# Fused attention and MLP block on one core: sequence rows 4p+j, loads in waves, and a new instruction order

## The chip, the cores and the metric

The kernel runs on 1 core of one Trainium2 chip. The metric is the device time of one execution in microseconds (us). Repeated executions of one kernel give a median and a range; each profiled execution also gives a span (first to last instruction, about 2 us less than the time) and the mean clock that was granted to TensorE. Engine names: PE is TensorE, PEld its weight loads, DVE VectorE, ACT ScalarE, POOL GpSimd, SP SyncE, which issues most DMAs.

## The reference

One transformer block on 2048 rows of 512 features, in bf16, with 32 heads. Each position attends to 8 positions: itself and those 2, 4, ... 14 before it.

```python
h   = x + attention(layernorm(x), wqkv) @ wo        # window 8, dilation 2
out = h + ((relu(n @ W_gate) * (n @ W_up)) @ W_down)  # n = layernorm(h), 1376 hidden features
```

## The kernel before

The rows are worked on in four chunks of 512. A chunk is loaded as four blocks of 128 rows, normalised, and transposed, so that the projections give q, k and v with the features on partitions and the positions along the free axis. The kernel adds all instructions to a plan; a list of ranks (tuned elsewhere) then fixes their order on every engine.

```python
x_rows   = A_x.rearrange("b (tb p) d -> p (b tb) d", p=P)        # block of 128 successive rows
out_rows = out.rearrange("b (tb p) d -> p (b tb) d", p=P)
...
kT = sb.tile([P, NT, PADL + S], BF16, name="kT")     # keys of all chunks in one tile, 16 columns of zeros ahead
vT = sb.tile([P, NT, PADL + S], BF16, name="vT")
...
# setup: every load is issued at once
for j in range(BPC):
    (nc.scalar if j % 2 else nc.sync).dma_start(x_sm[:, j:j + 1, :], x_rows[:, j:j + 1, :])
for c, q in enumerate((nc.sync, nc.scalar, nc.sync)):
    q.dma_start(w3_sb[c][:], w3_r[:, :, c * D:(c + 1) * D])
for tk in range(1, NCK):
    nc.sync.dma_start(x_sm[:, tk * BPC:(tk + 1) * BPC, :], x_rows[:, tk * BPC:(tk + 1) * BPC, :])
...
def f_ev(...):                       # eviction of a projection, 12 in each chunk, 48 in all
    if c == 0:
        o = qT.t[:, t, :]
    else:
        o = (kT if c == 1 else vT)[:, t, PADL + s0: PADL + s0 + CS]
    nc.scalar.copy(out=o, in_=mm.t[:])
...
def f_pr(...):                       # one score product: 2 feature tiles x 4 window positions x 512
    kb = kT[:, t:t + 2, PADL + s0 - 4 * hf * DIL: PADL + s0 - 4 * hf * DIL + CS]
    ...
    V.tensor_tensor(out=pb.t[:]..., in0=q4, in1=k4, op=ALU.mult)
```

The softmax here doesn't subtract the row's maximum and nothing guards it: scores larger than these inputs give would overflow.

## Time and profile before

| | |
|---|---|
| time, first three runs | 203.12 us (202.84 to 203.56) |
| time of the profiled execution | 205.38 us, span 203.6, clock 0.983 |
| the 48 projection evictions | 0.60 us each |

Beside the lines that the prediction shows, these two views matter later. The first is the page's busy times and the slices of ScalarE (40 equal slices, tenths of busy time):

```profile
PE 195.4 (96%) x1102; PEld 96.8 (48%) x1123; DVE 155.1 (76%) x246; ACT 127.7 (63%) x253; POOL 12.6 (6%) x26
...
ACT  3517879986569993797756599703665353576400
```

The second is the groups of the projection evictions (count, busy us and mean ns of one, idle time before them and its releaser):

```profile
L519 ACT CAST quad<-bank 128x512 bf16<-128x512 f32 x16 | 9.6, 601 | 7.4 <-PE bank L511 7.4
L519 ACT CAST vT<-bank 128x512 bf16<-128x512 f32 x16 | 9.5, 600 | 2.3 <-PE bank L511 2.3
L519 ACT CAST kT<-bank 128x512 bf16<-128x512 f32 x16 | 9.4, 599 | 3.3 <-PE bank L511 3.3
```

ScalarE is busy 63% on average, but several slices of the first half stand at 9.

### The profile page before, as it was taken

The numbers are of one execution on the slowest core, as the hardware profiler recorded it, in microseconds if no ns is written. First come the engines' busy times: TensorE is split into PE (matmuls) and PEld (weight loads), VectorE is DVE, ScalarE is ACT, GpSimd is POOL, SyncE is SP. The second block draws the span as 40 slices with busy tenths as digits, with TensorE's granted clock in tenths as the row PEclk, the third lists the DMA queues.
The fourth block names the chain that finished last, engine by engine and source line by source line (L and its number), as shares of the span: only waits on it lengthen the run. The fifth ranks groups of instructions, "written<-read, shape, count | busy, mean of one in ns | idle before, by whom it ended". The sixth has DMA issues, their size and how long they took to land.

```text
span 203.6 us, 2957 instructions
## 1 busy us (share of the span) xinstructions
PE 195.4 (96%) x1102; PEld 96.8 (48%) x1123; DVE 155.1 (76%) x246; ACT 127.7 (63%) x253; POOL 12.6 (6%) x26
## 2 busy tenths in 40 slices
PE   8499999999999999999999999999999999999994
PEld 8347545555545334444454444444444445444452
DVE  6549999999999999999999966599996255021314
ACT  3517879986569993797756599703665353576400
POOL 3000000330000002400033000000000000000000
PEclk9859999999999999999999999999999999999999
DMA  5999901698000002980059900400011001100003
GB/s 187 350 379 403 322 19 30 123 203 163 3 0 0 0 3 52 192 168 0 3 103 180 209 31 0 90 13 0 3 41 62 0 0 53 53 0 0 0 3 103
DMA packets 14893, 18.04 MB, mean 89 GB/s; under 512 B 5056, under 2 KB 12192, under 8 KB 14880
## 3 DMA queue, kind: packets, MB, share of 16 engines
q1 hardware_dynamic: 12336, 10.78, 16.4%
q0 software_dynamic: 1728, 6.29, 16.3%
q10 hardware_dynamic: 816, 0.79, 1.1%
q8 instruction: 9, 0.15, 0.3%
q14 instruction: 4, 0.03, 0.0%
HBM read 8.42 MB, written 2.10 MB: 52 GB/s over the span
## 4 chain that ended last, share of the span: by engine, by line
PE 93%; DMA 4%; issue 1%; SPq 0%; DVE 0%
PE bank L736 38%; PE bank L511 22%; PE bank L773 19%; PE bank L698 7%; DMA wq_sb<-in_A_wqkv_dram 4%; PE bank L564 4%; PE bank L465 2%; PE bank L625 1%; PE bank L597 1%; SPq L270 0%; DVE row L784 0%
## 5 line engine op out<-in xcount | busy, mean ns | idle before, releaser
L736 PE MATMUL bank<-quad,wg_sb 128*128 128x512 bf16 (+1 forms) x171 | 42.3, 379 | 0.3
L736 PE MATMUL bank<-quad,wu_sb 128*128 128x512 bf16 (+1 forms) x173 | 42.3, 379 | 0.1
L743 ACT ACTIVATE gr<-bank 128x512 bf16<-128x512 f32 (+1 forms) x44 | 26.0, 604 | 23.7 <-PE bank L736 18.3
L773 PE MATMUL bank<-wd_sb,gT 128*128 128x512 bf16 (+3 forms) x184 | 39.7, 366 | 0.2
L558 DVE TENSOR_TENSOR big<-quad,kT 128x4096 bf16<-128x4096 bf16 x16 | 36.0, 2284 | 0.1
L646 DVE TENSOR_TENSOR big<-big,vT 128x4096 bf16<-128x4096 bf16 x16 | 35.8, 2283 | 0.3 <-ACT big L631 0.3
L740 ACT CAST up_sb<-bank 128x512 bf16<-128x512 f32 (+1 forms) x44 | 25.7, 594 | 12.3 <-PE bank L736 8.5
L756 DVE TENSOR_TENSOR gT<-gr,up_sb 128x1024 bf16<-128x1024 bf16 (+1 forms) x24 | 15.4, 643 | 20.4 <-ACT gr L743 14.1
L773 PEld LDWEIGHTS <-gT 128*128 128x128 bf16 (+1 forms) x187 | 18.0, 98 | 19.3 <-issue 0.4
L736 PEld LDWEIGHTS <-wu_sb 128*128 128x128 bf16 (+1 forms) x176 | 17.3, 100 | 20.7 <-issue 1.3
L736 PEld LDWEIGHTS <-wg_sb 128*128 128x128 bf16 (+1 forms) x176 | 17.3, 100 | 20.6 <-issue 1.1
L511 PE MATMUL bank<-quad,wq_sb 128*128 128x512 bf16 (+1 forms) x70 | 16.9, 382 | 2.5 <-DMA wq_sb<-in_A_wqkv_dram 2.1
L631 ACT CAST big<-bank 128x512 bf16<-128x512 f32 x32 | 17.2, 610 | 1.5 <-PE bank L625 1.3
L511 PE MATMUL bank<-quad,wk_sb 128*128 128x512 bf16 (+1 forms) x70 | 16.8, 373 | 0.1
L678 POOL DMA_DIRECT2D big<-big x12 | 10.7, 894 | 98.3 <-DVE big L646 95.2
L784 DVE TENSOR_TENSOR row<-x_sm,bank 128x512 bf16<-128x512 bf16 (+1 forms) x17 | 10.6, 652 | 7.8 <-PE bank L773 7.8
L649 DVE TENSOR_TENSOR big<-big 128x1024 bf16<-128x1024 bf16 (+2 forms) x24 | 16.4, 727 | 0.0
L709 DVE SCALAR_TENSOR_TENSOR x_sm<-x_sm,bank 128x512 bf16<-128x512 bf16 x16 | 10.9, 685 | 6.8 <-PE bank L698 6.7
L511 PE MATMUL bank<-quad,wv_sb 128*128 128x512 bf16 x62 | 15.4, 379 | 0.1
L698 PE MATMUL bank<-wo_sb,quad 128*128 128x512 bf16 x61 | 14.8, 379 | 0.2
L371 ACT ACTIVATE row<-x_sm,mv 128x512 bf16<-128x512 bf16 x16 | 11.5, 717 | 4.5 <-DVE mv L363 4.4
L519 ACT CAST quad<-bank 128x512 bf16<-128x512 f32 x16 | 9.6, 601 | 7.4 <-PE bank L511 7.4
(65 smaller groups left out, 161.7 us busy)
## 6 DMA issues: line engine op xcount, KB each, us to landing
big<-big POOLq DMA_DIRECT2D x12, 512.0 KB, 5.5
out_dram<-row SPq DMA_DIRECT2D x15, 128.0 KB, 1.7
x_sm<-in_A_x_dram SPq DMA_DIRECT2D x3, 512.0 KB, 11.0
wu_sb<-in_B_W_up_dram SPq DMA_DIRECT2D x1, 1376.0 KB, 10.6
wg_sb<-in_B_W_gate_dram SPq DMA_DIRECT2D x1, 1376.0 KB, 13.9
wd_sb<-in_B_W_down_dram SPq DMA_DIRECT2D x1, 1280.0 KB, 15.7
wq_sb<-in_A_wqkv_dram SPq DMA_DIRECT2D x1, 512.0 KB, 8.4
wk_sb<-in_A_wqkv_dram ACTq DMA_DIRECT2D x1, 512.0 KB, 8.6
```

Of the source, the lines that this page charges most:

```text
L371: nc.scalar.activation(out=xn.t[:], in_=h.t[:] if h else x_sm[:, tk * BPC + j, :], func=ACT.Square, bias=mv.t[:, j, 0:1], scale=1.0, accum ...
L511: nc.tensor.matmul(mm.t[:, lo:hi], lhsT=w3_sb[c][:, dt, t:D:NT], rhs=xnT.t[:, dt, lo:hi], start=(dt == 0), stop=(dt == NT - 1))
L558: V.tensor_tensor(out=pb.t[:].rearrange("p (t w) s -> p t w s", t=2), in0=q4, in1=k4, op=ALU.mult)
L631: nc.scalar.copy(out=ab.t[:, w, :], in_=bc.t[:])
L646: V.tensor_tensor(out=mt.t[:], in0=ab.t[:], in1=v8, op=ALU.mult)
L649: V.tensor_tensor(out=mt.t[:, 0:n, :], in0=mt.t[:, 0:n, :], in1=mt.t[:, n:2 * n, :], op=ALU.add)
L698: nc.tensor.matmul(od.t[:], lhsT=OT.t[:, t, j * P:(j + 1) * P], rhs=wo_sb[:, t, :], start=(t == 0), stop=(t == NT - 1 and tk not in RPE))
L736: nc.tensor.matmul(mm.t[:fs, :], lhsT=w_sb[:, dt, ft * P: ft * P + fs], rhs=hnT.t[:, dt, :], start=(dt == 0), stop=(dt == NT - 1))
L740: nc.scalar.copy(out=ub.t[:fs, i, :], in_=um.t[:fs, :])
L743: nc.scalar.activation(out=gr.t[:fs, i, :], in_=gm.t[:fs, :], func=ACT.Relu)
L756: V.tensor_tensor(out=gt.t[:fs, 0:n, :], in0=gr.t[:fs, 0:n, :], in1=ub.t[:fs, 0:n, :], op=ALU.mult)
L773: nc.tensor.matmul(od.t[:, c0:c1], lhsT=gts[ft].t[:fs, ft % 2, j * P:(j + 1) * P], rhs=wd_sb[:fs, ft, c0:c1], start=(ft == 0), stop=(ft == ...
```

## The change

Its intent is to start the projections earlier and keep TensorE busy there. Each chunk is read so that partition p holds its rows 4p to 4p+3; load pieces become 2 KB per partition and more. Loads that are not needed at once wait behind tiny POOL copies. The first projections start on pieces of 128, 128 and 256 columns, with filler matmuls between them. Transposes of three norms (one more than before) go through DMA, the residual of chunk 0 is added by PE, and the second norm of chunk 0 runs in two groups. The order of all instructions is new.

With rows 4p+j a column block j of a projection holds positions 4c+j, so the eviction puts the positions in order by writing with a step of 4 elements.

```diff
-    x_rows = A_x.rearrange("b (tb p) d -> p (b tb) d", p=P)
-    out_rows = out.rearrange("b (tb p) d -> p (b tb) d", p=P)
+    x_rows = A_x.rearrange("b (tk p j) d -> p (b tk) j d", p=P, j=BPC)
+    out_rows = out.rearrange("b (tk p j) d -> p (b tk) j d", p=P, j=BPC)
...
+        for j, q in ((0, nc.sync), (2, nc.scalar)):
+            q.dma_start(x_sm[:, j:j + 2, :], x_rows[:, 0, j:j + 2, :])
+        for dt in range(NT):
+            (nc.scalar if dt % 2 else nc.sync).dma_start(wqk_sb[:, dt:dt + 1, :], w3_r[:, dt:dt + 1, 0:2 * D])
...
+        nc.gpsimd.tensor_copy(out=x_sm[0:1, BPC, 0:1], in_=x_sm[0:1, 0, 0:1])      # holds the next load back
+        nc.sync.dma_start(x_sm[:, BPC:2 * BPC, :], x_rows[:, 1, :, :])
+        nc.gpsimd.tensor_copy(out=wv_sb[0:1, 0, 0:1], in_=wqk_sb[0:1, 3, 0:1])
+        nc.sync.dma_start(wv_sb[:], w3_r[:, :, 2 * D:3 * D])
...
-    DACC = tuple((k, t) for k in range(3) for t in range(4))
+    DACC = tuple((k, t) for k in range(3) for t in range(4) if k or t < 2)
-    DMAT = (("h",2,0),("h",2,2),("x",3,0),("x",3,2))
+    DMAT = (('h',2,0),('h',2,2),('x',3,0),('x',3,2),('h',1,0),('h',1,2))
-    RPE, OPE = (), ()
+    RPE, OPE = (0,), ()
+    HG = ([[0, 1], [2, 3]], [[0, 1, 2, 3]], [[0, 1, 2, 3]], [[0, 1, 2, 3]])
...
-                nc.scalar.copy(out=o, in_=mm.t[:])
+                nc.scalar.copy(out=o.rearrange("p (c j) -> p j c", j=BPC),
+                               in_=mm.t[:].rearrange("p (j c) -> p j c", j=BPC))
...
-                    nc.tensor.matmul(od.t[:], lhsT=OT.t[:, t, j * P:(j + 1) * P], rhs=wo_sb[:, t, :],
+                    nc.tensor.matmul(od.t[:], lhsT=OT.t[:, t, j:CS:BPC], rhs=wo_sb[:, t, :],
```

Cut: the list of ranks, the scheduler's inner loop, the column pieces and fillers of the first projections, the removed ScalarE statistics of the fourth block, and estimates of durations.

## The prediction

> **What bounds the kernel now.** I read the page's slices first, since one core with one busy engine is the simplest story. These are the TensorE (PE), its granted clock (PEclk), and the DMA rate:
>
> ```profile
> PE   8499999999999999999999999999999999999994
> ...
> PEclk9859999999999999999999999999999999999999
> ...
> GB/s 187 350 379 403 322 19 30 123 203 163 3 0 0 0 3 52 192 168 0 3 103 180 209 31 0 90 13 0 3 41 62 0 0 53 53 0 0 0 3 103
> ```
>
> From slice 4 on PE is at 9 in every slice at a clock of 9: the kernel is PE bound, and no rearrangement of loads helps after about 16 us. What is not PE bound is the front: slice 2 has PE at 4, slice 3 has the clock at 5. So I took the chain of work that ended last, in order of time:
>
> ```profile
> 1.66 8.42 DMA wq_sb<-in_A_wqkv_dram
> 10.08 0.05 issue
> 10.13 2.32 PE bank L511 x9
> 12.45 0.22 issue
> 12.67 7.27 PE bank L511 x38
> ```
>
> The end hangs on the landing of wq at 10.08 us; from there on the chain is PE alone until 200.66. Then the windows of one us each around it (columns: window, length, busy PE, PEld, DVE, ACT, POOL with instruction counts, clock, DMA share, GB/s):
>
> ```profile
> 7.00:8.00 1.00, 1.00 (x14) 0.68 (x12) 1.00 (x4) 0.56 (x1) 0.00 (x0) 1.00 1.11 350
> 8.00:9.00 1.00, 0.05 (x1) 0.00 (x0) 0.26 (x1) 0.61 (x2) 0.00 (x0) 0.90 0.96 310
> 9.00:10.00 1.00, 0.00 (x0) 0.00 (x0) 0.00 (x0) 0.00 (x0) 0.00 (x0) 0.50 1.09 382
> 10.00:11.00 1.00, 0.87 (x5) 0.62 (x6) 0.00 (x0) 0.00 (x0) 0.00 (x0) 0.50 1.10 367
> ...
> 15.00:16.00 1.00, 1.00 (x5) 0.38 (x3) 1.00 (x6) 0.53 (x1) 0.00 (x0) 0.69 1.05 402
> 16.00:17.00 1.00, 1.00 (x7) 0.51 (x5) 1.00 (x2) 0.56 (x3) 0.00 (x0) 1.00 1.01 392
> ```
>
> All inputs of the first projections but the weights are there at 8.7; PE waits 2 us, and then works at half clock until 15.6 (0.69 in the last mixed window is 0.62 us of half clock). 10.13 to 15.62 at half clock is 5.5 us for 2.75 us of work. VectorE (DVE) is the second to look at, its timeline in the same stretch:
>
> ```profile
> 7.51 0.75 DVE L477 COPY quad<-bank 128x512 bf16<-128x512 bf16 x2
> 13.20 1.29 DVE L401 BATCH_NORM_STATS2 st<-x_sm 128x6 f32<-128x512 bf16 x2 [4.94 <-DMA x_sm<-in_A_x_dram]
> 14.40 0.17 DVE L404 BATCH_NORM_AGGREGATE mv<-st 128x2 f32<-128x6 f32 x1
> ```
>
> It idles 4.94 us for chunk 1 of x. Its first score product starts at 18.84, and from there to 110 us it has no idle time, so DVE is a bound in waiting: PE is kept busy only because projections of later chunks fill in.
>
> **What the Trainium skill says.** "TensorE: Matmul & The Clock Gate", Part 1 (the HAM clock gate): the clock falls to half after about 3.4 us without activity and returns after as much work. The trace agrees in kind: little PE work from 5.9, half clock by 8.9, full again at 15.6, 5.5 us after work resumed, more than one window. "DMA: Bandwidth & Descriptors", Queues, rings and completion order: queues share the same 16 engines and an engine takes turns between them at packet level, in ring order within one. It agrees: wq is 512 KB and landed 8.42 us after issue with the DMA share at 1.0, because wk, wv and x of later chunks moved beside it. Same page, Why small descriptors are slow: three cycles of overhead per packet on 32 B beats, by which I estimate 9% at 1 KB rows and 4.5% at 2 KB. The trace has 350 GB/s with 1 KB rows (5 to 8 us) and 402 once the 2752 B rows of wu move (15 to 16 us). "SBUF — State Buffer", Door 1: two accesses per 16 byte line keep full rate, so the new evictions with a step of 4 bf16 elements (8 bytes) should cost no more than the 0.60 us of the projection casts; no run shows it yet.
>
> **The change part by part.**
>
> *Loads in waves.* Ahead of the first projections only x chunk 0 (0.52 MB) and wq with wk (1.05 MB) are in the queues; chunk 1 and wv are held back by tiny POOL copies that wait for earlier landings. In the windows of before, 0.92 MB had moved by 5.0 us and 350 GB/s follow: 1.57 MB are through at 6.9 (a little earlier with 2 KB rows, a little later with the receipt). The other input, the first normalised block: x at about 3.75, statistics 0.65 and aggregate 0.13, Ln and Exp with hops 0.66 (16.98 to 17.55 in the trace of chunk 1), normalise 0.41, four transposes and their eviction 1.2: 6.8. First projection at 6.9 instead of 10.13: -3.2. Before, the Exp stood behind a 0.7 us Square on ACT; that pair is removed.
>
> *Clock.* 44 warm-up matmuls of 103 ns end at 5.5; transposes, two fillers of 8 matmuls and 128-column pieces keep PE busy some 70% from there to 10.5. I expect no half clock: -2.75, and the 0.22 issue gap goes: -0.2.
>
> *PE work after the first projection.* Counted from the instruction orders, 512 columns at 0.216 us: four identity matmuls for the residual of chunk 0 +0.86; 16 transposes of chunk 1's second norm gone to DMA -0.90; 8 transposes and 8 fillers now fall after the start +0.90. Sum +0.86.
>
> *First residual on PE* takes 4 x 0.685 us off DVE (row L709), ACT evicts instead. *No DMA accumulate for two tiles of chunk 0* gives 2 x 1.22 us back (row L649, 128x2048) but spares a 5.5 us transfer. DVE is level. *Second norm in two groups* lets the first half of chunk 0 be transposed earlier. By the orders, DVE reaches chunk 0's last output tile at about 48.8 against 53.1, and PE comes to its output projection at about 49: no long wait.
>
> *New waits.* Three pieces (128, 128, 256 columns) need all four blocks. In the new DVE order two statistics of chunk 1 stand between the last normalisations, so summing rows puts the 256 piece at 10.5 where PE's own work would be there at 9.6: +0.9. From there the first score product starts at 14.2 (before 18.84). The DVE order then holds four products of 2.2, five statistics of 0.62, aggregates and one normalisation before the mask: 12.9 us, so the first spread of weights cannot start before 27.2, when PE would be there at 26.5: up to +0.85. The same count puts chunk 1's output tiles at 86.7 against PE at 86.2: up to +0.5. I charge 0.8 for these two together, since the order was plainly tuned and my hops are rough.
>
> Sum: -3.2 - 2.75 - 0.2 + 0.86 + 0.9 + 0.8 = -3.6, from 203.1 to 199.5 us. The tail after the last matmul (0.42 us addition, store of 1.6) is unchanged.
>
> **The rivals.** (1) DVE becomes the bound: the front gains nearly 6 us on PE, but the DVE chain starts only 4.6 us earlier and carries more before the first spread. For it: DVE is gapless from 18.84 to 110; against: after 120 its share falls to 60%, so a wait can only arise before. All waits in full and one more us: 201. (2) The front comes out as designed and the waits do not bind, since projections of later chunks can stand in: only -3.2, -2.75, -0.2, +0.86 count, 197.8. (3) The clock falls anyway, because the pieces come in drips between 6.9 and 10.5: half clock over three or four us costs 1.5 to 2, 201.3. Against it: PE's longest gap would be under 1 us. (4) The gain is given back in DMA: DMA transposes issue at 1.2 us each on SP and land after 2.5; four more for chunk 1 must be done before 102 us and are, by the order, at 100.6. If late: +1 to 2.
>
> **Range and chances.** The 2% line is at 199.06, within half a us of the sum, so the chances are nearly even with the waits deciding; that nothing is saved would need a fault in several parts. 199.5 us, 8 in 10 between 197.7 and 201.2; faster by over 2% 0.40, within 2% 0.58, slower 0.02.
>
> **What would show it.** First projection at 6.7 to 7.1 and no window with a clock under 0.95 after 6 us: the first two terms. The 256-column piece near 10.5 with PE idle about 1 us between 8 and 10.7, released by ACT or DVE: the third. DVE products from about 14.2; PE idle before the first spread near 27 and before output projections of chunk 1 near 86. Projection casts at 0.60 us: the strided write is free. Wrong would be: a half-clock window, wq with wk landing after 7.5, or PE idle time of over 2 us after 20.

## The result, and the profile after

The changed kernel takes **229.4 us** (228.44 to 230.67, six runs) against 203.13 (202.71 to 204.5) of the kernel before. The ratio is 1.1286 (95% interval 1.1239 to 1.1333).

The page of the changed kernel, in the same rows:

```profile
PE 204.1 (90%) x1139; PEld 98.8 (43%) x1139; DVE 155.9 (69%) x241; ACT 154.5 (68%) x259; POOL 11.0 (5%) x26
...
PE   7899568988896588999999999899999999999992
...
ACT  3499599999999999669963459672067383067700
...
PEclk9999976999999959999999999999999999999998
...
PE 45%; ACT 31%; DVE 12%; DMA 8%; issue 3%; POOL 0%; ACTq 0%; DVEq 0%; POOLq 0%
...
L535 ACT CAST kT<-bank 128x512 bf16<-128x512 f32 x16 | 22.0, 1395 | 2.9 <-DVE big L575 2.2
L535 ACT CAST vT<-bank 128x512 bf16<-128x512 f32 x16 | 22.6, 1430 | 0.0
L535 ACT CAST quad<-bank 128x512 bf16<-128x512 f32 x16 | 21.8, 1421 | 0.0
```

Three things are to be seen. The evictions went from 0.60 to about 1.42 us each. They are preceded by hardly any idle time: ScalarE goes from one to the next. And ScalarE now carries 31% of the chain that ended last, which before was TensorE alone from 10 us on. The windows from 30 to 80 us show how full it is (columns: window, length, busy PE, PEld, DVE, ACT, POOL, clock, DMA share, GB/s). After:

```profile
30.00:40.00 10.00, 7.06 (x40) 2.29 (x38) 4.05 (x14) 10.00 (x15) 0.00 (x0) 0.77 0.23 41
40.00:60.00 20.00, 17.92 (x89) 8.81 (x88) 17.73 (x22) 19.97 (x23) 1.87 (x2) 1.00 0.31 59
60.00:80.00 20.00, 14.90 (x84) 6.21 (x83) 10.71 (x13) 20.00 (x34) 0.00 (x0) 0.98 0.00 1
```

Before, in the same windows:

```profile
30.00:40.00 10.00, 9.95 (x63) 5.47 (x61) 10.00 (x18) 9.85 (x22) 1.60 (x2) 1.00 0.32 63
40.00:60.00 20.00, 19.89 (x104) 9.87 (x104) 19.45 (x30) 13.73 (x27) 1.99 (x3) 1.00 0.53 102
60.00:80.00 20.00, 19.72 (x151) 8.50 (x152) 20.00 (x15) 16.86 (x35) 0.86 (x1) 1.00 0.00 1
```

ScalarE is busy for all of these 50 us, while TensorE and VectorE wait; in 30 to 40 us the clock falls to 0.77 on top. The front, in contrast, came out much as designed. TensorE's timeline there:

```profile
7.35 1.04 PE L526 MATMUL bank<-quad,wqk_sb 128*128 128x128 bf16 x12
...
10.98 3.20 PE L526 MATMUL bank<-quad,wqk_sb 128*128 128x256 bf16 x22 [0.23 <-ACT quad L501]
```

The first projection stands at 7.35 us (before 10.13), the piece of 256 columns at 10.98, and the clock is at full until past 20 us. VectorE's first score product is already late:

```profile
16.73 2.29 DVE L575 TENSOR_TENSOR big<-quad,kT 128x4096 bf16<-128x4096 bf16 x1 [2.12 <-ACT quad L535]
```

It starts 2.5 us later than the 14.2 of the prediction and idles 2.12 us for an eviction of line 535. Without the stepped write, in the runs below, it starts at 14.0 to 14.5.

### The profile page after: what moved, and what is told of

Read it like the earlier page. It is cut to its first block, busy times and chain, and to the rows that moved or that the text cites. A ratio compares the mean times of both kernels' runs of the same rounds, so it can differ in the third digit from the quotient of the medians.

```text
span 227.2 us, 3001 instructions
## 1 busy us (share of the span) xinstructions
PE 204.1 (90%) x1139; PEld 98.8 (43%) x1139; DVE 155.9 (69%) x241; ACT 154.5 (68%) x259; POOL 11.0 (5%) x26
## 4 chain that ended last, share of the span: by engine, by line
PE 45%; ACT 31%; DVE 12%; DMA 8%; issue 3%; POOL 0%; ACTq 0%; DVEq 0%; POOLq 0%
PE bank L753 20%; PE bank L790 17%; ACT quad L535 7%; ACT kT L535 6%; ACT vT L535 6%; PE bank L715 5%; DVE big L575 4%; DMA big<-big 4%; DVE big L663 4%; DMA x_sm<-in_A_x_dram 3%; ACT big L648 2%; ACT quad L501 2%; ACT up_sb L757 2%; PE bank L581 1%; ACT gr L760 1%
## 5 line engine op out<-in xcount | busy, mean ns | idle before, releaser
L526 PE MATMUL bank<-quad,wqk_sb 128*128 128x512 bf16 (+2 forms) x160 | 33.4, 348 | 2.9 <-ACT quad L535 1.4
L526 PEld LDWEIGHTS <-wqk_sb 128*128 128x128 bf16 x160 | 16.3, 115 | 17.9 <-issue 8.9
L535 ACT CAST kT<-bank 128x512 bf16<-128x512 f32 x16 | 22.0, 1395 | 2.9 <-DVE big L575 2.2
L535 ACT CAST vT<-bank 128x512 bf16<-128x512 f32 x16 | 22.6, 1430 | 0.0
L535 ACT CAST quad<-bank 128x512 bf16<-128x512 f32 x16 | 21.8, 1421 | 0.0
L666 DVE TENSOR_TENSOR big<-big 128x1024 bf16<-128x1024 bf16 (+2 forms) x26 | 19.1, 767 | 3.0 <-DMA big<-big 3.0
L648 ACT CAST big<-bank 128x512 bf16<-128x512 f32 x32 | 18.2, 651 | 1.0 <-PE bank L642 1.0
L526 PE MATMUL bank<-quad,wv_sb 128*128 128x512 bf16 x64 | 17.7, 410 | 0.8 <-ACT vT L535 0.4
L801 DVE TENSOR_TENSOR row<-x_sm,bank 128x512 bf16<-128x512 bf16 (+1 forms) x17 | 10.5, 651 | 11.1 <-PE bank L790 11.1
L456 DVE TENSOR_SCALAR row<-x_sm,mv,rs 128x512 bf16<-128x512 bf16 x32 | 11.7, 403 | 7.3 <-ACT rs L438 7.3
```

The costliest lines, as they stand in the source:

```text
L526: nc.tensor.matmul(mm.t[:, lo:hi], lhsT=wv_sb[:, dt, t:D:NT] if c == 2 else wqk_sb[:, dt, c * D + t:(c + 1) * D:NT], rhs=xnT.t[:, dt, lo:h ...
L535: nc.scalar.copy(out=o.rearrange("p (c j) -> p j c", j=BPC), in_=mm.t[:].rearrange("p (j c) -> p j c", j=BPC))
L648: nc.scalar.copy(out=ab.t[:, w, :], in_=bc.t[:])
L666: V.tensor_tensor(out=mt.t[:, 0:n, :], in0=mt.t[:, 0:n, :], in1=mt.t[:, n:2 * n, :], op=ALU.add)
```

## The experiments

### 1. What does the stepped write cost, and where does the cost sit?

**Plain evictions in the changed kernel**, with a wrong result (positions out of order):

```diff
-                nc.scalar.copy(out=o.rearrange("p (c j) -> p j c", j=BPC),
-                               in_=mm.t[:].rearrange("p (j c) -> p j c", j=BPC))
+                nc.scalar.copy(out=o, in_=mm.t[:])
```

> The changed kernel with its 48 projection evictions written without a step (wrong result on purpose: q, k and v then stand in the order of the row blocks). Theory S, the stepped write is the whole loss: in the changed kernel the 48 casts take 1.42 us each against 0.60 before, 39 us of ScalarE; here they are back at 0.60 and the kernel at 197 to 201 us, as the rest of the prediction had it. Rival R, the new order leaves VectorE or the clock as the bound and the slow casts only fill idle ScalarE: the casts fall to 0.60 but the kernel stays over 212 us.

Measured: 208.98 us, ratio 1.0264 (1.023 to 1.0298), evictions 0.598 to 0.617 us. The step is worth 20.4 us, but 5 us more than before remain, and the prediction stays far off. The time lies between the two theories: the step is most of the loss and not all of it.

**The changed kernel with the old rows**, which needs no step and is correct:

```diff
+    x_rows = A_x.rearrange("b (tk j p) d -> p (b tk) j d", p=P, j=BPC)
+    out_rows = out.rearrange("b (tk j p) d -> p (b tk) j d", p=P, j=BPC)
+                nc.scalar.copy(out=o, in_=mm.t[:])
+    ... lhsT=OT.t[:, t, j * P:(j + 1) * P]
```

> The changed kernel with the old rows (block of 128 successive rows), so plain evictions and plain weights of the output projection, all else as changed; correct result. Theory S: 197 to 201 us, within 1 us of the plain-eviction run; the x rows of 1 KB in place of 4 KB cost under 0.5 us, since the first wave has the same bytes. If instead the 4 KB rows are worth something, x lands later and this run is 1 us or more above the plain-eviction run. Rival R: over 212.

Measured: 208.95 us (208.44 to 210.94), ratio 1.0285. It agrees with the first run: between these two, the new rows themselves gain or cost nothing that can be seen.

**The kernel before with the new rows alone**, stepped evictions included, correct:

```diff
-                nc.scalar.copy(out=o, in_=mm.t[:])
+                nc.scalar.copy(out=o.rearrange("p (c j) -> p j c", j=BPC),
+                               in_=mm.t[:].rearrange("p (j c) -> p j c", j=BPC))
```

> The kernel before with the new rows alone (rows 4p+j, stepped evictions, stepped weights of the output projection, x loads in 4 KB runs for chunks 1 to 3); correct result. Theory S: casts at about 1.4 us, ScalarE bound up to 70 us, 218 to 235 us. Rival R (the order is to blame): 202 to 206 us, whatever the casts take. A third cause, the stepped weights of the output projection, would show as a weight load above 0.10 us.

Measured: 222.07 us, ratio 1.0922 (1.088 to 1.0964), evictions 1.398 to 1.425 us. So the step costs some 18 us in the old order as well. 48 evictions of 0.82 us more are 39 us of ScalarE; about half of it comes through. That the rest lies in ScalarE's idle time is argued, not measured. The third cause that the expectation named is there too: the weight loads of the output projection, read with a step of 4, take 0.114 us instead of 0.098. It does not show in the time: the run with plain evictions has these loads at 0.114 us, the one with the old rows at 0.098, and they take 208.98 and 208.95 us.

**The step moved to the reading side.** The eviction writes SBUF in order and reads PSUM with a step of 128 fp32; rows 4p+j are kept, and the result is correct:

```diff
-                nc.scalar.copy(out=o.rearrange("p (c j) -> p j c", j=BPC),
-                               in_=mm.t[:].rearrange("p (j c) -> p j c", j=BPC))
+                nc.scalar.copy(out=o.rearrange("p (c j) -> p c j", j=BPC),
+                               in_=mm.t[:].rearrange("p (j c) -> p c j", j=BPC))
```

> The changed kernel with the same permutation put on the other side of the eviction: PSUM is read with a step of 128 elements and SBUF written without a step; correct result. If the stepped write to SBUF is what is slow (S-write): casts at 0.60 to 0.70 us, 197 to 202 us. If ScalarE is slow on any pattern that is not one run (S-any): casts at 1.2 us or more, over 218 us.

Measured: 209.89 us (208.35 to 210.96), evictions 0.598 to 0.625 us, as S-write has it; the time lies outside both ranges, for the reasons of part 2. The same permutation is free on the PSUM side and costs 0.82 us on the SBUF side. This also makes it a mere matter of the order in which the loops are written.

**Other steps**: q with a step of 2 elements, k with 8, v with none. Its output is wrong, which doesn't matter for the time.

```diff
+                n = (2, 8, 1)[c]
+                nc.scalar.copy(out=o.rearrange("p (c j) -> p j c", j=n),
+                               in_=mm.t[:].rearrange("p (j c) -> p j c", j=n))
```

> The changed kernel with a different step in the write of each projection's eviction (wrong result on purpose): q with a step of 2 elements (4 bytes), k with 8 elements (16 bytes), v without a step. What is read is the duration of the three casts; with 4 elements (8 bytes) it was 1.42 us and without a step 0.60. If the cost is per written element as soon as elements don't touch (theory P): q and k both at about 1.4 us. If it goes with how many elements share a line of 16 bytes (theory L): q well under 1.4, 0.6 to 0.9, and k above it, 2 us or more. v at 0.60 to 0.65 in both.

Measured (durations of one in ns: least, median, greatest; q is written to quad):

```profile
L536 ACT CAST kT<-bank x16: 2419/2490/2897, 13.0 to 82.8; 128x512 bf16<-128x512 f32 x16
L536 ACT CAST quad<-bank x16: 723/812/1107, 17.6 to 76.4; 128x512 bf16<-128x512 f32 x16
L536 ACT CAST vT<-bank x16: 563/650/992, 31.2 to 111.3; 128x512 bf16<-128x512 f32 x16
```

A step of 1, 2, 4, 8 bf16 elements thus takes 0.60 (0.65 for v in this run), 0.81, 1.41 and 2.49 us. With a step of n the write passes over the row n times, so it touches a 16-byte piece 64, 128, 256 and 512 times. The differences are 0.16 to 0.21, 0.60 and 1.08 us for 64, 128 and 256 more touches: 2.5 to 5 ns for each. That fits a cost for every visit of a 16-byte line, and not the rule that the prediction took from the Trainium skill, that two hits on a line are enough for full rate: at step 4 each line is hit twice in a row. That the line is the mechanism is read from four sizes, not measured by itself.

**VectorE**: in the kernel before, its final addition (reads PSUM) and its normalisation (SBUF to SBUF) write with a step of 4. Its output is wrong, which doesn't matter for the time.

```diff
-                    V.tensor_tensor(out=ob.t[:, c0:c1], in0=x_sm[...], in1=od.t[:, c0:c1], op=ALU.add)
+                    V.tensor_tensor(out=ob.t[:, c0:c1].rearrange("p (c j) -> p j c", j=4),
+                                    in0=x_sm[...].rearrange("p (j c) -> p j c", j=4),
+                                    in1=od.t[:, c0:c1].rearrange("p (j c) -> p j c", j=4), op=ALU.add)
```

(The normalisation likewise.)

> The kernel before with two VectorE operations that write with a step of 4 bf16 elements, 32 and 15 times (wrong result on purpose; scalar evictions untouched at 0.60 us): the final addition, which reads PSUM (row<-x_sm,bank, 0.683 us in the kernel before), and the normalisation, SBUF to SBUF (row<-x_sm,mv,rs, 0.408 us). If the cost per 16-byte line belongs to the write into SBUF whatever the engine, both take 1.2 to 1.6 us. If it belongs to ScalarE alone: the addition stays at 0.65 to 0.75, and the normalisation is 0.4, or up to about 0.7 if it loses a faster mode[...]. The kernel's time: about 204 to 206 in the second case, over 210 in the first.

Measured: 213.45 us beside 202.64 of the kernel before. The groups in this run:

```profile
L436 DVE TENSOR_SCALAR row<-x_sm,mv,rs 128x512 bf16<-128x512 bf16 x32 | 21.8, 842 | 3.0 <-ACT rs L418 3.0
L785 DVE TENSOR_TENSOR row<-x_sm,bank 128x512 bf16<-128x512 bf16 x15 | 18.4, 1321 | 6.3 <-PE bank L774 6.3
```

In the kernel before they took 0.408 and 0.683 us. So VectorE pays too, 0.64 us more in the addition. The normalisation, at 0.842, lies between the two expectations (1.2 to 1.6, and up to 0.7). How much of its 0.43 is the write and how much a faster mode that it may have lost is not told apart.

### 2. Where are the remaining 9 us over the prediction?

Without the step the change takes 209 us, and 199.5 had been predicted. Two candidates: the loads do not give what was hoped, or the new order has waits of its own.

**Loads as before**, put back into the version with plain rows (all issued at once, wq and wk whole):

```diff
-        ... loads in waves, held back by two gpsimd.tensor_copy
+        for j in range(BPC):
+            (nc.scalar if j % 2 else nc.sync).dma_start(x_sm[:, j:j + 1, :], x_rows[:, 0, j:j + 1, :])
+        nc.sync.dma_start(wqk_sb[:, :, 0:D], w3_r[:, :, 0:D])
+        nc.scalar.dma_start(wqk_sb[:, :, D:2 * D], w3_r[:, :, D:2 * D])
+        nc.sync.dma_start(wv_sb[:], w3_r[:, :, 2 * D:3 * D])
+        for tk in range(1, NCK): ...
```

> The block-row version of the changed kernel (208.95 us in the first call) with the loads of before: no waves, q and k weights in one piece of 512 KB each, wv and all of x queued at once; correct result. If the waves do what the prediction said, the first projection goes from about 7 us to about 10 us and the clock falls to half for 3 to 6 us: PE reaches the same point 4 to 6 us later, and the kernel takes 211 to 214 us. If the later waits of the order swallow the front, it stays at 208 to 210.

Measured: 214.71 us (213.47 to 215.75), 5.8 us more than with waves, a little over the range. The first projection is at 9.44 us there and the clock is at half from about 9.3 to 12.7. But part of the 5.8 us goes with half clock later on. Both profiles have a later stretch at half clock (clock 0.83 in 60 to 70 us with waves, in 70 to 80 without), and between them the last matmul differs by 3.3 us (it ends at 204.34 and 207.59). Four of the six executions with waves had a clock of 0.994 to 0.997, which leaves no room for that stretch; the four without waves had 0.983 or less. Whether that stretch follows from the loads or is a draw is open, so in this order the waves are worth 3 to 6 us; the prediction gave them 6.

**Waves alone in the kernel before**, rows and order untouched:

```diff
+        for j, q in ((0, nc.sync), (2, nc.scalar)):
+            q.dma_start(x_sm[:, j:j + 2, :], x_rows[:, j:j + 2, :])
+        for c in range(2):
+            nc.sync.dma_start(w3_sb[c][:, 0:2, :], w3_r[:, 0:2, c * D:(c + 1) * D])
+            nc.scalar.dma_start(w3_sb[c][:, 2:4, :], w3_r[:, 2:4, c * D:(c + 1) * D])
+        ... chunk 1 and wv held back as in the change
```

> The kernel before with the loads in waves alone (x chunk 0, then q and k weights in four pieces of 256 KB; chunk 1 and wv held back by the two tiny POOL copies); rows, evictions, order of all engines as before; correct result. If the front terms of the prediction are right by themselves (first projection 2 us earlier at about 8.1, as the normalised blocks are ready then, and no half clock, 2.75): 198 to 199.5 us. If the front is swallowed later because VectorE bounds the middle: 201 to 203.

Measured: 202.49 us (202.28 to 202.74), ratio 0.9949 (0.9922 to 0.9976): the fastest kernel, but the gain is 1.0 us, where 4 or more had been expected. The first projection stands at 8.58 us instead of 10.13, 1.55 us earlier; there is no gain beyond that. The expected rest, the half clock, was hardly there to be saved. The 26 timed executions of the kernel before that ran beside the experiments list their mean clock: 17 have 0.998 or more (mean time 203.58 us), 8 have 0.989 to 0.992 (203.98), and one has 0.983 (205.46), like the profiled execution that the prediction was read from (0.983, 205.38). The long half-clock stretch of that profile is an uncommon draw. Where it occurs it goes with 1.8 to 1.9 us more, not 2.75: the two executions at 0.983 took 205.38 and 205.46, the 17 at full clock 203.58.

**The shared key tile.** The profile of the version with plain rows shows a stall of TensorE at 63.9 to 67.2 us. ScalarE's timeline there:

```profile
61.29 0.58 ACT L535 CAST vT<-bank 128x512 bf16<-128x512 f32 x1
63.54 0.59 ACT L535 CAST kT<-bank 128x512 bf16<-128x512 f32 x1 [1.67 <-DVE big L574]
64.03 0.60 ACT L616 ACTIVATE lnd<-bank 128x512 f32<-128x512 f32 x1
64.66 0.63 ACT L619 ACTIVATE rec<-lnd 128x512 bf16<-128x512 f32 x1
65.19 1.91 ACT L501 COPY quad<-bank 128x1024 bf16<-128x1024 bf16 x2
```

VectorE's:

```profile
61.17 2.29 DVE L574 TENSOR_TENSOR big<-quad,kT 128x4096 bf16<-128x4096 bf16 x1
65.32 0.76 DVE L628 TENSOR_TENSOR ex<-ex,rec 128x512 bf16<-128x512 bf16 x2 [1.87 <-ACT rec L619]
```

TensorE's:

```profile
65.80 0.40 PE L641 MATMUL bank<-ex,spread 32*128 32x512 bf16 x4 [1.88 <-DVE ex L628]
67.15 1.44 PE L752 MATMUL bank<-quad,wu_sb 128*128 128x512 bf16 x3 [0.96 <-ACT quad L501]
```

Read it backwards. TensorE waits for the reciprocal and the copies of ScalarE; those stand behind a key eviction; that eviction waits 1.67 us until a score product ends at 63.46. The product reads the keys of the chunk before, the eviction writes those of the next chunk: nothing forces that wait but that both touch one tile, and with two feature rows in the product's access the ranges overlap. TensorE idles 2.8 us here and then runs at half clock (0.83 in 60 to 70 us). The half clock does not always follow: the run with the step on the PSUM side has the same two waits (1.88 and 0.96 us), and its profile shows a clock of 1.00 there. The edit gives each chunk its own key tile and copies the 16 columns that reach back:

```diff
-    kT = sb.tile([P, NT, PADL + S], BF16, name="kT")
+    kTs = [sb.tile([P, NT, PADL + CS], BF16, name=f"kT{i}_") for i in range(NCK)]
...
+                if c == 1 and s0 + CS < S:
+                    nc.gpsimd.tensor_copy(out=kTs[s0 // CS + 1][:, t, 0:PADL], in_=kTs[s0 // CS][:, t, CS:CS + PADL])
```

The first attempt was spoiled. To find room, the operand of the warm-up matmuls was placed in the tile of the last weights, so they waited for its load.

> The block-row version of the changed kernel with k transposed in four tiles, one per chunk, in place of one tile (POOL copies the 16 last columns of each chunk to the next tile); correct result. In the block-row run two evictions of k waited for a VectorE product that reads another chunk of the same tile, at 24.1 and 63.5 us, and ScalarE and then PE stood still behind them (PE idle about 1.3 and 2.8 us, with half clock for about 3 us after the second). Theory W, these two waits are false dependencies within one tile and cost the time: both waits are gone, 203 to 205 us. Rival D, VectorE is late anyway and PE waits for its products and norms: 207 to 209.

Measured: 230.51 us. The waits say why: "PE bank L375 <- DMA wd_sb<-in_B_W_down_dram", 27.5 us. Nothing follows from it but that a borrowed buffer brings its waits along. The second attempt borrows an activation buffer that no load touches:

> The kernel with plain rows (208.95 us) with the transposed keys in four tiles, one for each chunk, the 112 columns that reach back copied by GpSimd; the warm-up matmuls read a corner of a gT buffer, so they no longer wait for a load. Correct. Theory W (the key evictions of the next chunk wait for score products of the chunk before only because both touch one tile, and behind them the in-order ScalarE holds everything): the waits of kT evictions on the big products go, TensorE does not stall at 62 to 67 us, and the time is 202 to 204.5 us. Rival D (TensorE is short of VectorE's products there anyway): 207 to 209.5 us, with PE waiting for DVE instead.

(That text speaks of 112 columns; it is 16.) Measured: 205.37 us (205.05 to 206.15), 3.6 us less than with one tile, ratio 1.0092. The waits of key evictions on products are gone and the result is correct, so they were not needed. It is 0.9 us above the expected range, hence theory W holds but is not the whole rest.

**The same with rows 4p+j undone on the PSUM side**, that is the whole change as it was meant, without its two faults:

> The same four key tiles in the kernel that keeps the rows 4p+j and undoes the order on the PSUM side (209.89 us): the whole change as it was meant, with neither the stepped write nor the shared tile. Correct. Theory W: within 1 us of the run with plain rows and four tiles, so 202 to 205 us; if the 4 KB rows are worth anything at the start or end, 0.5 us less than that one. Rival D: 208 to 210.

Measured: 204.62 us (204.47 to 204.8), ratio 1.0045 (1.0011 to 1.008), as theory W has it. That is 5.3 us less than with one tile; but two of the four executions with one tile had a clock of 0.987 or 0.988 (210.48 and 210.96) and two 0.995 (208.35 and 209.31), and against the latter the gain is about 4 us, near the 3.6 with plain rows. It is also 0.75 us less than with plain rows and four tiles, more than the 0.5 that was to speak for the new rows; the intervals of the two ratios overlap, so this is a hint and not shown. TensorE still idles 1.1 us in 60 to 70 us, behind ScalarE, which is busy 9.97 of these 10 us; the clock stays at 1.00.

**The four tiles in the kernel before with waves:**

> The kernel before with loads in waves (202.49 us, ratio 0.995) and four key tiles. Correct. Before had no long wait of a kT eviction on a product, so theory W expects no more than 0.5 us of gain: 201.8 to 203 us. If the shared tile cost something in that order too that the waits do not show, 200 to 201.5.

Measured: 208.05 us (204.9 to 208.23); the profiled run and one other count as slow, the interval of the ratio is wide (1.0032 to 1.0233), and no gain is to be seen: even the fastest run is above 202.49. What the fastest lacked is not known, since only a slow one has a profile; that profile shows the reason of its own stall. POOL's timeline:

```profile
34.47 6.84 POOL L527 COPY kT__80<-kT__79 128x16 bf16<-128x16 bf16 x2 [7.87 <-ACT kT__79 L525]
41.24 1.01 POOL L686 DMA_DIRECT2D big<-big  x1
```

and VectorE's:

```profile
32.22 8.89 DVE L654 TENSOR_TENSOR big<-big,vT 128x4096 bf16<-128x4096 bf16 x4
...
48.62 1.36 DVE L657 TENSOR_TENSOR big<-big 128x1024 bf16<-128x1024 bf16 x3 [2.12 <-DMA big<-big]
```

POOL also issues the DMAs that accumulate the attention output. The copies of 16 columns stood in its queue, waiting for their key evictions, and one of the two above took 6.7 us for 128x16 elements (spans on POOL are rough). The accumulations behind them came late, VectorE waited, and TensorE idled 3.38 us before 55.35. The Trainium skill, "SBUF — State Buffer", section "Who interferes with whom", says that a VectorE instruction with two SBUF inputs contends with a GpSimd instruction that reads SBUF. The trace agrees: such copies took 0.2 us at the least, and the long ones ran beside products of 2.29 us with two SBUF inputs and ended as these ended. The one above ended at 41.17, the row of four products beside it at 41.12; an earlier one took 8.96 us, from 16.56 to 25.52, beside a row of four that ended at 25.45. The mend is good for the order that needs it, and not for the other.

### 3. The tail

After its last matmul (198.03 us) the version above took 4.5 us to the end of the span; the kernel before takes 2.9. The prediction had called the tail unchanged. The program's order of SyncE's queue, with which instruction waits for VectorE, shows the last five stores in another order than the additions they store (row names; additions row0, row3, row1, row4, row2). It is no view of the profile; the trace agrees with it in the stores' sizes and waits, and the five start one after the other from 197.84, when the fourth addition has ended (197.81):

```
36 L807 DMACopy out<-row4 128x512 [waits DVE]
37 L807 DMACopy out<-row3 128x512
38 L807 DMACopy out<-row1 128x256
39 L807 DMACopy out<-row0 128x512
40 L807 DMACopy out<-row2 128x256 [waits DVE]
```

The first store waits for the fourth addition and holds up three that were ready; the fifth queues behind all. The edit gives the last stores the ranks in the order of their additions:

```diff
+    ranks = sorted(s.prio for s in outs.values())
+    for key, rank in zip(sorted(adds, key=lambda k: adds[k].prio), ranks):
+        outs[key].prio = rank
```

> The kernel with rows 4p+j undone on the PSUM side and four key tiles (204.62 us, ratio 1.0045), with only the last five stores of the output put in the order in which VectorE finishes their rows. Correct. In that kernel the last matmul ended at 198.03 us and the span at 202.5, 4.5 us later; in the kernel before the same tail is 2.9 us, because there the stores stand in the order of the additions. Theory T (the order of the stores in the queue of SyncE holds four of them until the fourth addition, and the last one queues behind them): the tail becomes 2.9 to 3.1 us and the time 203.0 to 203.4 us, ratio 0.996 to 0.999. Rival (the tail is longer because of the rows 4p+j or of the DMA itself): no change, 204.4 to 204.8.

Measured: 203.56 us (203.18 to 204.11), ratio 0.997 (0.9916 to 1.0024). The issues of the last five stores, first without the edit:

```profile
197.84 2.29 SPq L807 DMA_DIRECT2D out_dram<-row  x5
```

and with it:

```profile
196.23 2.91 SPq L807 DMA_DIRECT2D out_dram<-row  x5
```

They now begin as the first addition ends (196.21). The tail is 3.2 us after the last matmul, which ends at 198.34, instead of 4.5; 2.9 to 3.1 had been expected. The time falls by 1.1 us in place of the expected 1.2 to 1.6. The two ratios were taken in different sessions and their intervals overlap, so theory T rests on the profile's tail more than on the times.

### What the runs show together

| kernel | us | ratio to before |
|---|---|---|
| before | 203.1 to 204.0 (medians of the sessions) | 1 |
| before with waves | 202.49 | 0.9949 |
| before with new rows and stepped writes | 222.07 | 1.0922 |
| the change | 229.4 | 1.1286 |
| - step on the PSUM side | 209.89 | 1.0302 |
| - and four key tiles | 204.62 | 1.0045 |
| - and stores in the order of the additions | 203.56 | 0.997 |

## Why the prediction was wrong

**The step that failed** is the sentence that the new evictions "should cost no more than the 0.60 us of the projection casts". They cost 1.40 to 1.43, and moving the step to the PSUM side takes 19.5 us off with nothing else changed (20.4 with plain evictions). The prediction had marked it as shown by no run, yet gave it no width: no rival had ScalarE as the bound, and the chance of slower was 0.02. Two of its own signs of being wrong came true: TensorE idles 2.78 us before 27.49, and the clock falls in 30 to 40 us (0.77). The numbers for a warning were in the profile before: 48 evictions times a possible doubling are 29 us on an engine that stood at 9.85 of 10 us in the window from 30 to 40 us.

**The sum, term by term.**

- *First projection, -3.2.* It came at 7.35 us instead of 10.13: 2.8 by the start; the weights landed at about 7.3, where 6.9 was predicted. In the kernel before, waves alone moved it by 1.55 us and the time by 1.0; in the new order they are worth 3 to 6. Right as to mechanism, somewhat too large.
- *Clock, -2.75.* Mis-sized. The half clock did not come back in the front, as predicted. But it was sized from one execution that was itself 2.2 us over the median, and then taken off the median. Among 26 executions one had as low a clock, and the two known at that clock took 1.8 to 1.9 us more, not 2.75. For the median there was little to save.
- *The issue gap (-0.2)* was not isolated, nor were the single parts of the +0.86 of PE work, the DMA accumulations and the norm in two groups.
- *The 256-column piece, +0.9.* It stood at 10.98, not 10.5; close. Just ahead of it TensorE idled 0.23 us; between 8 and 11 it idled 0.41, where about 1 had been expected.
- *Waits, +0.8.* Half right in place, wrong in cause. Without the stepped write TensorE does wait before the first spread, 0.71 us at 27.7 (27.2 and up to 0.85 predicted), but with four key tiles that wait is gone: VectorE was late there because of the shared tile. Near 86 there is no wait. The false wait through the shared tile cost about 4 us in all (3.6 with plain rows, 5.3 with rows 4p+j, some of it clock); 1.1 us of stall at 62 us remain after its removal. Rival 1 looked for the bound on VectorE; it was ScalarE's order. (VectorE was also not quite gapless from 18.84 to 110: the windows from 40 to 60 us show it idle for 0.54.)
- *The tail, "unchanged".* It was 4.6 us instead of 2.9, of which the order of the stores explains 1.3 (4.5 to 3.2 in the profiles).

**The ledger.** From 229.4 us, the step takes 19.5, the shared tile 5.3, the stores 1.1; 203.6 remain. That is 4.1 above the prediction. As an estimate from the profiles, 2.75 are a clock gain that the median did not hold, 0.4 to 0.7 the first projection (7.27 and 7.60 in the two profiles with rows 4p+j and four tiles, 6.9 predicted) and 0.3 the tail (3.2 instead of 2.9). The remaining stall of 1.1 stands in place of the 0.8 that had been charged for waits, 0.3 more, and up to 0.4 stay open. These differences are of medians from several sessions on more than one chip, with the kernel before at 203.1 to 204.0, so the last few tenths mean nothing. Even mended, the change gains nothing that is clear of zero; its one part that does, the loads in waves, gains 0.5% by itself.

## What to carry to other kernels

Where a permutation must be made in an eviction by ScalarE, put the step on the PSUM side and write SBUF in order (VectorE was not tried with the step on that side); and before a change adds cost to every instruction of a group, multiply it by the count and compare it with that engine's fullest windows, not with its average. Compare a profile with the spread of the timed runs before sizing a gain from it: a stretch that only that execution has cannot be saved from the median. When a new order is made, read the queues for an instruction that waits for something later than those behind it: one tile for all chunks and stores out of order both did that here.

## What the Trainium skill lacked or had wrong

- "SBUF — State Buffer", Door 1 (cachelines): two hits on each 16-byte line, and steps of up to 8 bf16, are said to keep full rate. ScalarE's writes of 128x512 took 0.60, 0.81, 1.41 and 2.49 us at steps of 1, 2, 4 and 8 bf16; only step 1 was at full rate. VectorE's addition went from 0.683 to 1.321 us at step 4, and weight loads of 128x128 that read with a step of 4 took 0.114 us, not 0.098.
- "PSUM — Partial Sum Buffer", Specifications (cachelines): it speaks of non-contiguous patterns that slow matmuls. It lacks that ScalarE's reads with a step of 128 fp32 cost nothing here: 0.598 to 0.625 us against 0.60.
- "TensorE: Matmul & The Clock Gate", Part 1: it lacks how often a front like this one falls into half clock. Among 26 executions of the kernel before the mean clock was 0.998 or more in 17, 0.989 to 0.992 in 8 and 0.983 in one; and after the same stall of 2.8 us one profile shows half clock and another none.
- "SBUF — State Buffer", Who interferes with whom: no duration is given for small GpSimd copies under contention; one of 128x16 bf16 took from 0.2 to 8.96 us, the longest as long as a row of four VectorE products of 2.29 us.
